# The layer-2 routing of a fused attention and expert kernel: VectorE steps with one operand in PSUM

## The chip, the cores and the metric

The kernel runs on one core of a Trainium2 chip. Five engines of that core work side by side, each through its own list of instructions in order: TensorE (PE; its weight loads are listed as PEld), VectorE (DVE), ScalarE (ACT), GpSimd (POOL), and SyncE (SP), which here only starts DMAs. They wait for one another through semaphores. SBUF is the working memory of 128 partitions. PSUM is the smaller memory into which TensorE writes its results: eight banks of 512 fp32 numbers in each partition, which VectorE and ScalarE also read and write, and POOL and the DMAs do not.

The metric is the device time of one execution in microseconds (us). Before the change it is 998.45 us, the median of three runs (997.95, 998.45 and 1000.06).

## The reference, cut to what matters

Three layers follow each other. The first is attention with a memory term (4 batches, 8 heads, 576 positions, head size 64). Its output, 2304 tokens of 512 numbers, goes through an expert layer in which each token has one of eight experts (512 to 1024 to 512 with a relu). The result goes through a second expert layer in which each token has two. The change concerns how the second layer chooses those two experts. Cut to that:

```python
def _moe2_ref(x, w_gate, w_noise, noise, w1, w2):
    logits = x @ w_gate
    noise_scale = np.log1p(np.exp(x @ w_noise))
    noisy_logits = logits + noise_scale * noise
    top2 = np.argpartition(-noisy_logits, 2, axis=1)[:, :2]
    top2_l = np.take_along_axis(noisy_logits, top2, axis=1)
    top2_w = np.exp(top2_l - top2_l.max(-1, keepdims=True))
    top2_w /= top2_w.sum(-1, keepdims=True) + 1e-09
    for e in range(E):
        for k in range(2):
            mask = top2[:, k] == e
            h = np.maximum(x[mask] @ w1[e], 0.0)
            out[mask] += top2_w[mask, k, None] * (h @ w2[e])
```

## The kernel before, in words

The attention runs first (about 0 to 220 us), its order fixed by a planner in `Tasks` that the change leaves alone. Then `layer1` works through the first expert layer in units of 256 token slots, each unit with the weights of one expert. `full` handles one unit, and `pair` handles two half-filled experts. In this data the order is one `full`, one `pair`, and then seven `full` (the number of pairs and of units is read at run time, in `tc.If` branches). Then `layer2` takes the eight experts of the second layer in turn with up to 640 slots each.

**One unit of layer 1.** Weights and tokens are split into a high and a low part of reduced precision, so each product is three matmuls. `mm1` (L706) makes one of eight blocks of the hidden layer, f = 0 to 7: twelve matmuls (L712 to L714) into a PSUM bank of the kind `h`, then ACT writes the high part `hh` (L715), then DVE writes the low part `hl` from the bank and `hh` (L717). There are two `h` banks, so block f can begin only when `hl` of block f-2 has read its bank. Between the blocks `split_w` (L685) splits the second weight matrix: ACT writes `w2h` (L687), and DVE or POOL writes `w2l` (L688), for f = 3, 5, 7 on DVE and otherwise on POOL. Then `mm2` (L718) makes the output in eight pieces (L722 to L724), between which `split_w1` (L689) splits the next unit's first matrix (L691 on ACT, L692 on DVE and POOL alternately) and `rows` turns the next unit's tokens (L702 to L704).

**The routing of layer 2 rides along.** As soon as a unit's output is known, its tokens' experts of layer 2 are chosen during the next unit. `logits` (L743) computes the two products of the reference (L748, L753, L758) and puts them into the table `L` (L759). `route2` (L869) is a generator of some forty very small DVE steps (16 to 32 numbers in a partition, later 192 to 768) with a few steps of ACT, POOL and PE. `pump` (L760) issues a few of them at a time after each block: five per place in layer 1 (`PUMP`), eight in layer 2 (`PUMP2`). The steps are:

- L878 to L892: softplus of the noise logits by a series, times the noise, plus the logits
- L894 to L899: the two largest, their experts, and the sum `A` of the two one-hot rows
- L901 to L905: PE counts ranks from `A` into a bank of the kind `sm`; this part is held until a given place of the unit
- L906 to L923: the weights of the two experts, each token's slot and column
- L925 to L928: one-hot tables `ol` and `rr` (named `rrm` in the rows) in which slot number and weight are spread out
- L931 and L934: PE multiplies the two, and DVE adds the result to the table `M2`. This last part of a unit is issued after block 1 of the unit behind (`behind`, or at the end of `layer2`'s own chain)

All of these tables stand in SBUF. The order of instructions on each engine is the order in which the code issues them (`manual_schedule`). `Banks` gives each kind of PSUM tile two of the eight banks in turn: `h` 0 and 1, `y` 2 and 3, `tp` (transposes) 4 and 5, `sm` 6 and 7. The attention uses banks 6 and 7 for its own purposes first.

In `layer2` the last unit's routing stands on the way: its `rr` has to be added to `M2` before the list of each expert's tokens is known, so its steps are pumped eight at a time into the first blocks of the first expert.

At L780 (behind the pair) and L785 (behind the last unit) the branches end. There an engine may go on only when the engines it depends on have come to the same place.

Of the kernel before, what the change touches and what calls it, by code (L numbers as in the profile page):

```python
# [9 lines left out]
FT=mybir.dt.float32; FR=mybir.dt.float32r; I32=mybir.dt.int32  # L10
# [275 lines left out]
col=lambda u: 2*u if u<2 else FC+2*(u-2)  # L286
# [12 lines left out]
class Banks:  # L299

    def __init__(s, pool):
        s.all=[pool.tile([128,512],FT,name='b%d'%i) for i in range(8)]
        s.of=dict(h=[0,1],y=[2,3],tp=[4,5],sm=[6,7]); s.n=dict.fromkeys(s.of,0)
    def tile(s, shape, dt, name):
        b=s.all[s.of[name][s.n[name]%2]]; s.n[name]+=1
        return b.rearrange('p (a c) -> p a c',a=shape[1]) if len(shape)==3 else b

class Moe:
    def __init__(s, ctx, tc, ident, consts, areas):
# [40 lines left out]
    def blocks(s, nc, c, areas):  # L350

        def T(j, o, w, name, dt=FT):
            assert o+w<=AREAS[j]
            return nc.alloc_sbuf_tensor_at(name,[128,w],dt,offset=nc.lookup_mloc(areas[j]).addr+4*o).ap()
        cut=lambda j,o,w,name,n,dt=FT:[T(j,o+i*w,w,name+str(i),dt) for i in range(n)]
        V=lambda a,k: a.rearrange('p (k w) -> p k w',k=k)
        K0,K1,X,HL,W2,G,X1,OL=range(8)
        s.w1r=V(T(K0,0,4096,'w1r'),KD); s.w2r=V(T(K0,4096,4096,'w2r'),KF); s.os=cut(K0,8192,512,'os',2)
        s.w1h=V(T(K1,0,4096,'w1h',FR),KD); s.w1l=V(T(K1,4096,4096,'w1l',FR),KD); s.yt=V(T(K1,8192,1024,'yt'),KD); s.rr=c.tile([128,4,256],FR,name='rrm')
        s.xh=V(T(X,0,2560,'xh',FR),KD); s.xl=V(T(X,2560,2560,'xl',FR),KD)  # L360
        s.w2h=cut(W2,0,512,'w2h',KF,FR); s.w2l=cut(W2,4096,512,'w2l',KF,FR)
        H=lambda n: [T(HL,o,KF*n,x+str(n),FR).rearrange('p (f c) -> p f c',f=KF) for o,x in ((0,'hh'),(5120,'hl'))]
        s.hidden=dict(l1=H(UT),l2=H(C2)); s.hh,s.hl=s.hidden['l1']
# [15 lines left out]
        for r in (0,64):  # L379
            nc.gpsimd.affine_select(m4[r:r+64,half-64:],m4[r:r+64,half-64:],pattern=[[-1,64]],compare_op=OP.is_ge,fill=-8e9,base=0,channel_multiplier=1)  # L380
    def banks(s):
        b=s.ps.all; s.bufs.update(s=b[:4],pt=b[4:6],m=b[6:7],ot=b[7:])

    def bias(s, Q, A, ids, mbias):

# [7 lines left out]
        for m in range(nm):  # L393
# [335 lines left out]
    def state(s):  # L729
        nc=s.nc; c=s.c  # L730
        s.run=c.tile([128,E],FT,name='run'); nc.gpsimd.memset(s.run,float(DEAD))
        s.M2=c.tile([128,4,NC2],FT,name='M2'); nc.gpsimd.memset(s.M2,0.0)

        s.NV=NF+NP2+1
        s.sv=c.tile([128,s.NV,2,4],FT,name='sv'); nc.gpsimd.memset(s.sv,8000.0)
        s.val=c.tile([128,s.NV,4,4],FT,name='val'); nc.gpsimd.memset(s.val,0.0)
        s.nz=c.tile([128,3,2,E],FT,name='nz')
        s.L=c.tile([128,2,2*E],FT,name='L'); s.nx=c.tile([128,2,2],FT,name='nx'); s.nxi=c.tile([128,2],I32,name='nxi'); s.lp=c.tile([128,UT],FT,name='lp')
        s.uxi=c.tile([128,2,NF],I32,name='uxi'); s.cnt=c.tile([128,2],I32,name='cnt')
        s.last=c.tile([128,NF],FT,name='last')  # L740
        s.gn=c.tile([128,NF,2],FT,name='gn'); s.gh=c.tile([128,NP2+1,2],FT,name='gh'); s.gni=c.tile([128,NF,2],I32,name='gni')
        s.gsi=c.tile([128,NP2+1,2],I32,name='gsi')
# [126 lines left out]
    def route2(s, wk, ps, u, nt):  # L869

        nc=s.nc; V=nc.vector; G_=nc.gpsimd
        T=lambda name,sh,dt=FT: wk.tile(sh,dt,name=name+('' if nt==2 else '_'))
        cur=s.tabs[:,COLS:COLS+nt]; nz=s.nz[:,2,:nt]; J=2*nt
        G=s.L[:,:nt,:E]; Z=s.L[:,:nt,E:]
        SH=[128,nt,E]
        vals=s.val[:,u,:J]; sv=s.sv[:,u,:,:J]

        e_=T('e_',SH); V.scalar_tensor_tensor(e_,Z,-1.0,Z,op0=OP.mult,op1=OP.min)  # L878
        nc.scalar.activation(e_,e_,AF.Exp); yield
        for k in range(2): G_.tensor_copy(vals[:,nt*k:nt*k+nt,0:2],cur[:,:,0:2])  # L880
# [12 lines left out]
        mx=T('mx2',SH); ix=T('ix2',SH,U32); OH=T('OH',[128,2,nt,E]); id_=T('id_',[128,2,nt])
        for t in range(nt): V.max(mx[:,t],n[:,t]); yield  # L894
        for t in range(nt): V.max_index(ix[:,t],mx[:,t],n[:,t]); yield
        kt=lambda x:x[:,:,0:2].rearrange('p t k -> p k t')
        V.tensor_add(id_,kt(ix),cur[:,None,:,2].to_broadcast([128,2,nt])); yield
        V.tensor_tensor(OH,s.io[:,None,None,:E].to_broadcast([128,2,nt,E]),id_[:,:,:,None].to_broadcast([128,2,nt,E]),op=OP.is_equal); yield
        A=T('A2',SH,BF); V.tensor_add(A,OH[:,0],OH[:,1]); yield 1  # L899
        rp=ps.tile([128,512],FT,name='sm')  # L900
        nc.tensor.matmul(rp[:,0:E],s.trib,A[:,0],start=True,stop=True)  # L901
        if nt==2:
            nc.tensor.matmul(rp[:,E:2*E],s.trib,A[:,1],start=True,stop=False)
            nc.tensor.matmul(rp[:,E:2*E],s.onesb,A[:,0],start=False,stop=True)
        for t in range(nt): nc.tensor.matmul(rp[:,nt*E:(nt+1)*E],s.onesb,A[:,t],start=t==0,stop=t==nt-1)  # L905
        V.tensor_scalar(sv[:,1],id_.rearrange('p k t -> p (k t)'),float(TS),None,op0=OP.mult); yield  # L906
        d=T('d2',[128,nt]); V.tensor_sub(d,mx[:,:,1],mx[:,:,0])
        nc.scalar.activation(d,d,AF.Exp); yield
        rk=T('rk',SH)
        V.tensor_add(rk,rp[:,:nt*E].rearrange('p (t e) -> p t e',t=nt),s.run[:,None,:].to_broadcast(SH)); yield  # L910
        V.tensor_add(s.run,s.run,rp[:,nt*E:(nt+1)*E]); yield
        W=T('w_',[128,J]); V.tensor_scalar(W[:,:nt],d,1.0,1e-9,op0=OP.add,op1=OP.add); yield
        tmp=T('tmp',[128,2,nt,E]); V.tensor_mul(tmp,OH,rk[:,None].to_broadcast([128,2,nt,E])); yield
        V.reciprocal(W[:,:nt],W[:,:nt]); yield
        r=T('r4',[128,J],I32)
        with nc.allow_low_precision(reason='a sum of one whole number and zeros'):
            V.tensor_reduce(r,tmp.rearrange('p k t e -> p (k t) e'),axis=AX.X,op=OP.add)
        yield
        V.tensor_mul(W[:,nt:],W[:,:nt],d); yield
        wh=T('wh',[128,J],FR); G_.tensor_copy(wh,W); G_.tensor_copy(vals[:,:,2],wh.bitcast(FT)); G_.tensor_sub(wh,W,wh.bitcast(FT)); G_.tensor_copy(vals[:,:,3],wh.bitcast(FT))  # L920
        ri=T('ri',[128,2,J],I32); s.lohi(ri,r); yield
        G_.tensor_copy(sv[:,0],r)
        col=T('col',[128,J]); V.scalar_tensor_tensor(col,ri[:,1],float(T2),sv[:,1],op0=OP.min,op1=OP.add); yield  # L923
        ol=s.ol2[:,:J]
        V.tensor_tensor(ol,s.io[:,None,:].to_broadcast([128,J,128]),ri[:,0,:,None].to_broadcast([128,J,128]),op=OP.is_equal); yield  # L925
        oc=wk.tile([128,4,NC2],FT,name='oc')[:,:J]; rr=s.rr[:,:J,:4*NC2].rearrange('p j (a c) -> p j a c',a=4); B=[128,J,4,NC2]
        V.tensor_tensor(oc,s.io[:,None,:NC2].to_broadcast([128,J,NC2]),col[:,:,None].to_broadcast([128,J,NC2]),op=OP.is_equal); yield
        V.tensor_mul(rr,oc[:,:,None].to_broadcast(B),vals[:,:,:,None].to_broadcast(B)); yield 2  # L928
# [218 lines left out]
```

## Time and profile before

| | |
|---|---|
| median of three runs | 998.45 us |
| the profiled execution | 994.96 us, of which 993.2 us are the span from the first to the last instruction |
| PE busy | 949.5 us, 96% of the span |
| PEld busy | 835.0 us, 84% |
| DVE busy | 568.4 us, 57% |
| ACT busy | 487.7 us, 49% |
| POOL busy | 352.8 us, 36% |
| mean granted clock of TensorE | 0.983 of full speed |

An engine's busy time is the sum of its instructions' spans, so a VectorE instruction that has started and stands still counts as busy. "Idle before" in a row is the time in which the engine did nothing ahead of that instruction, and the arrow names what released it. [...] The end of a matmul is modelled: consecutive matmuls of 256 columns start every 0.12 us while each shows 0.28 us, so an idle time that the rows give ahead of such a matmul is 0.16 us shorter than what PE lost.

### The profile page before, as it was taken

The numbers are of one execution on the slowest core, as the hardware profiler recorded it, in microseconds if no ns is written. First come the engines' busy times: TensorE is split into PE (matmuls) and PEld (weight loads), VectorE is DVE, ScalarE is ACT, GpSimd is POOL, SyncE is SP. The second block draws the span as 40 slices with busy tenths as digits, with TensorE's granted clock in tenths as the row PEclk, the third lists the DMA queues.
The fourth block names the chain that finished last, engine by engine and source line by source line (L and its number), as shares of the span: only waits on it lengthen the run. The fifth ranks groups of instructions, "written<-read, shape, count | busy, mean of one in ns | idle before, by whom it ended". The sixth has DMA issues, their size and how long they took to land. (4 is left out here: it accounts for less than half of the span.)

```text
span 993.2 us, 18544 instructions
## 1 busy us (share of the span) xinstructions
PE 949.5 (96%) x6849; PEld 835.0 (84%) x6849; DVE 568.4 (57%) x1675; ACT 487.7 (49%) x1141; POOL 352.8 (36%) x411
## 2 busy tenths in 40 slices
PE   7999999999998999999988999999999999999994
PEld 5888888888876888888867889898989989898983
DVE  8777776899853888888865344253342424244310
ACT  6887878784433555555532243343343434344320
POOL 4222232245634567666644311221313012131111
PEclk9999999999998999999989999999999999999998
DMA  7345856363585455556653334535546353534212
GB/s 208 97 113 186 264 190 194 113 228 101 158 310 186 154 207 195 177 192 210 213 174 128 87 106 135 131 76 135 142 105 153 111 121 106 160 77 110 29 23 35
DMA packets 83842, 144.99 MB, mean 146 GB/s; under 512 B 14480, under 2 KB 32912, under 8 KB 83728
## 3 DMA queue, kind: packets, MB, share of 16 engines
q1 hardware_dynamic: 73168, 117.10, 35.8%
q0 software_dynamic: 10560, 26.47, 13.5%
q8 instruction: 60, 0.98, 0.4%
q14 instruction: 54, 0.44, 0.1%
HBM read 111.65 MB, written 31.97 MB: 145 GB/s over the span
## 5 line engine op out<-in xcount | busy, mean ns | idle before, releaser
L712 PE MATMUL b<-xh,w1h 128*128 128x304 f32 (+3 forms) x800 | 242.1, 303 | 10.4 <-DVEq L785 4.7
L713 PE MATMUL b<-xl,w1h 128*128 128x304 f32 (+3 forms) x800 | 239.5, 299 | 2.8 <-DVEq L780 2.6
L714 PE MATMUL b<-xh,w1l 128*128 128x304 f32 (+3 forms) x800 | 238.6, 298 | 0.8 <-POOLq L780 0.8
L717 DVE SCALAR_TENSOR_TENSOR hl<-b,hh 128x304 fp32r<-128x304 f32 (+3 forms) x200 | 90.3, 452 | 215.2 <-ACT hh L715 215.2
L722 PE MATMUL b<-w2h,hh 128*128 128x512 f32 x464 | 189.1, 407 | 0.0
L724 PE MATMUL b<-w2h,hl 128*128 128x512 f32 x464 | 182.4, 393 | 0.0
L723 PE MATMUL b<-w2l,hh 128*128 128x512 f32 x464 | 181.9, 392 | 0.0
L955 POOL DMA_INDIRECT out_dram<-os,l2s x40 | 63.7, 1593 | 327.6 <-ACT os L954 248.9
L715 ACT ACTIVATE hh<-b 128x304 fp32r<-128x304 f32 (+3 forms) x200 | 81.8, 409 | 187.6 <-PE b L714 187.4
L712 PEld LDWEIGHTS b<-xh,w1h 128*128 128x128 f32 x800 | 153.8, 192 | 18.0 <-DVE hl L717 9.2
L713 PEld LDWEIGHTS b<-xl,w1h 128*128 128x128 f32 x800 | 154.1, 193 | 3.8 <-DVEq L780 2.8
L714 PEld LDWEIGHTS b<-xh,w1l 128*128 128x128 f32 x800 | 154.1, 193 | 1.1 <-POOLq L780 1.1
L724 PEld LDWEIGHTS b<-w2h,hl 128*128 128x128 f32 x464 | 87.6, 189 | 19.7
L723 PEld LDWEIGHTS b<-w2l,hh 128*128 128x128 f32 x464 | 88.2, 190 | 15.7
L722 PEld LDWEIGHTS b<-w2h,hh 128*128 128x128 f32 x464 | 88.0, 190 | 15.6
L151 ACT ACTIVATE p<-sm,l 128x128 f32<-128x128 f32 (+4 forms) x144 | 84.1, 592 | 17.2 <-DVE l L147 17.2
L687 ACT CAST w2h<-w2r 128x512 fp32r<-128x512 f32 x128 | 78.5, 613 | 0.0
L704 DVE TENSOR_TENSOR xl<-b,xh 128x512 fp32r<-128x512 f32 x56 | 38.4, 688 | 69.9 <-ACT xh L703 69.9
L703 ACT CAST xh<-b 128x512 fp32r<-128x512 f32 x56 | 32.8, 587 | 90.1 <-PE b L702 90.1
L954 ACT ACTIVATE os<-b,l2w 128x512 f32<-128x512 f32 x40 | 27.6, 691 | 99.3 <-PE b L724 46.6
L691 ACT CAST w1h<-w1r 128x512 fp32r<-128x512 f32 x128 | 74.7, 619 | 0.0
L692 POOL TENSOR_TENSOR w1l<-w1r,w1h 128x512 fp32r<-128x512 f32 x44 | 59.1, 1352 | 42.3 <-ACT w1h L691 41.2
(500 smaller groups left out, 1536.2 us busy)
## 6 DMA issues: line engine op xcount, KB each, us to landing
w1r<-in_w_dram SPq DMA_DIRECT2D x18, 2048.0 KB, 9.7
w2r<-in_w_dram SPq DMA_DIRECT2D x18, 2048.0 KB, 9.1
xd<-gs SPq DMA_DIRECT2D x24, 260.0 KB, 3.7
xd<-x SPq DMA_DIRECT2D x10, 520.0 KB, 10.1
out_dram<-gs SPq DMA_DIRECT2D x19, 256.0 KB, 3.8
k<-in_k_dram SPq DMA_DIRECT2D x16, 256.0 KB, 4.4
q<-in_q_dram SPq DMA_DIRECT2D x16, 256.0 KB, 3.7
v<-in_v_dram SPq DMA_DIRECT2D x16, 256.0 KB, 4.3
```

The lines of the kernel that those rows point to most:

```text
L151: s.nc.scalar.activation(s.P[b,i,u][:,lh*n:lh*n+n],s.SM[b,i,u][:,lh*n:lh*n+n],AF.Exp,scale=-1.0,bias=L[:,0,c:c+1],accum_out=L[:,1,c:c+1])
L687: nc.scalar.copy(hi[c],raw[:,c])
L691: nc.scalar.copy(s.w1h[:,:,fs],s.w1r[:,:,fs])
L712: nc.tensor.matmul(h[:,:n],s.w1h[:,k,fs],s.xh[:,k,cs],start=k==0,stop=False)
L713: nc.tensor.matmul(h[:,:n],s.w1h[:,k,fs],s.xl[:,k,cs],start=False,stop=False)
L714: nc.tensor.matmul(h[:,:n],s.w1l[:,k,fs],s.xh[:,k,cs],start=False,stop=k==KD-1)
L715: def mm1_a(s, h, f, c0, n): s.nc.scalar.activation(s.hh[:,f,c0:c0+n],h[:,:n],AF.Relu)
L717: cs=slice(c0,c0+n); s.nc.vector.scalar_tensor_tensor(s.hl[:,f,cs],h[:,:n],0.0,s.hh[:,f,cs].bitcast(FT),op0=OP.max,op1=OP.subtract)
L722: nc.tensor.matmul(y,s.hh[:,f,cs],s.w2h[f],start=f==0,stop=False)
L723: nc.tensor.matmul(y,s.hh[:,f,cs],s.w2l[f],start=False,stop=False)
L724: nc.tensor.matmul(y,s.hl[:,f,cs],s.w2h[f],start=False,stop=f==KF-1)
L955: nc.gpsimd.indirect_dma_start(out=out,out_offset=bass.IndirectOffsetOnAxis(ap=si[:,c:c+1],axis=0),in_=o,in_offset=None,compute_op=OP.add)
```

## The change

`s.of['sm']` shrinks to bank 6 alone, and bank 7 becomes a work area for the routing. In it stand `L` (the logits) and the tables `q_`, `acc`, `rk`, `id_`, `col` and `oc` of `route2`. `e_`, `rg`, `q2`, `qn`, `n_`, `OH`, `tmp` and the rest stay in SBUF. Two instructions are new: a copy `zs` of the noise logits in SBUF, so that L878 has one operand in each memory, and a second product `qs`, which puts q times e into SBUF beside the one in PSUM, for the square that follows. The sum `A` of the two one-hot rows becomes a reduction with a single input. The bank that takes the product of L931 is now one of the kind `tp`, because `sm` has only one left.

```diff
-        s.of=dict(h=[0,1],y=[2,3],tp=[4,5],sm=[6,7]); s.n=dict.fromkeys(s.of,0)
+        s.of=dict(h=[0,1],y=[2,3],tp=[4,5],sm=[6]); s.n=dict.fromkeys(s.of,0)
     def tile(s, shape, dt, name):
-        b=s.all[s.of[name][s.n[name]%2]]; s.n[name]+=1
+        b=s.all[s.of[name][s.n[name]%len(s.of[name])]]; s.n[name]+=1
...
-        b=s.ps.all; s.bufs.update(s=b[:4],pt=b[4:6],m=b[6:7],ot=b[7:])
+        b=s.ps.all
+
+        def V(o,*sh):
+            a=b[7][:,o:o+math.prod(sh)]
+            return a if len(sh)==1 else a.rearrange('p (a b) -> p a b',a=sh[0])
+        s.L=V(0,2,2*E); s.pv=dict(q_=V(32,2,E),acc=V(48,2,E),rk=V(64,2,E),id_=V(80,2,2),col=V(84,4),oc=V(128,4,NC2))
+        s.bufs.update(s=b[:4],pt=b[4:6],m=b[6:7],ot=b[7:])
...
-        T=lambda name,sh,dt=FT: wk.tile(sh,dt,name=name+('' if nt==2 else '_'))
+        assert nt==2
+        T=lambda name,sh,dt=FT: s.pv[name] if name in s.pv else wk.tile(sh,dt,name=name)
...
-        e_=T('e_',SH); V.scalar_tensor_tensor(e_,Z,-1.0,Z,op0=OP.mult,op1=OP.min)
+        e_=T('e_',SH); zs=T('zs',SH); V.tensor_copy(zs,Z); V.scalar_tensor_tensor(e_,Z,-1.0,zs,op0=OP.mult,op1=OP.min)
...
-        V.tensor_mul(q,q,e_); yield
-        q2=T('q2',SH); V.tensor_mul(q2,q,q); yield
+        qs=T('qs',SH); V.tensor_mul(qs,q,e_); V.tensor_mul(q,q,e_); yield
+        q2=T('q2',SH); V.tensor_mul(q2,q,qs); yield
...
-        A=T('A2',SH,BF); V.tensor_add(A,OH[:,0],OH[:,1]); yield 1
+        A=T('A2',SH,BF)
+        with nc.allow_low_precision(reason='a sum of zeros and ones'): V.tensor_reduce(A,OH.rearrange('p k t e -> p t e k'),axis=AX.X,op=OP.add)
+        yield 1
...
-        oc=wk.tile([128,4,NC2],FT,name='oc')[:,:J]; rr=s.rr[:,:J,:4*NC2].rearrange('p j (a c) -> p j a c',a=4); B=[128,J,4,NC2]
+        oc=T('oc',[128,4,NC2]); rr=s.rr[:,:J,:4*NC2].rearrange('p j (a c) -> p j a c',a=4); B=[128,J,4,NC2]
...
-        mp=ps.tile([128,512],FT,name='sm')
+        mp=ps.tile([128,512],FT,name='tp')
```

On VectorE nothing else moves past these steps. Between blocks 4 and 5 of the first expert of layer 2, VectorE had this order before the change (`hl640` is the low part of the hidden block, `b0` and `b1` are the `h` banks, `L` the logits):

```order
L717 SCALAR_TENSOR_TENSOR hl640_88<-b0_155,hh640_87 128x224
L878 SCALAR_TENSOR_TENSOR e__8192<-L_231 128x16
L881 SCALAR_TENSOR_TENSOR rg_8197<-L_231,nz_230 128x16
L882 TENSOR_TENSOR rg_8197<-rg_8197,L_231 128x16
L883 TENSOR_SCALAR q__8200<-e__8192 128x16
L884 RECIPROCAL q__8200<-q__8200 128x16
L885 TENSOR_TENSOR q__8200<-q__8200,e__8192 128x16
L886 TENSOR_TENSOR q2_8204<-q__8200 128x16
L887 TENSOR_TENSOR qn_8206<-q__8200,nz_230 128x16
L717 SCALAR_TENSOR_TENSOR hl640_88<-b1_156,hh640_87 128x224
L688 TENSOR_TENSOR w2l5_82<-w2r_60,w2h5_74 128x512
L888 TENSOR_SCALAR acc_8224<-q2_8204 128x16
```

The same place after the change, where `b7` is the work area in PSUM and the line numbers are those of the changed kernel:

```order
L723 SCALAR_TENSOR_TENSOR hl640_88<-b0_155,hh640_87 128x224
L885 COPY zs_8160<-b7_162 128x16
L885 SCALAR_TENSOR_TENSOR e__8159<-b7_162,zs_8160 128x16
L888 SCALAR_TENSOR_TENSOR rg_8166<-b7_162,nz_230 128x16
L889 TENSOR_TENSOR rg_8166<-rg_8166,b7_162 128x16
L890 TENSOR_SCALAR b7_162<-e__8159 128x16
L891 RECIPROCAL b7_162<-b7_162 128x16
L892 TENSOR_TENSOR qs_8171<-b7_162,e__8159 128x16
L892 TENSOR_TENSOR b7_162<-b7_162,e__8159 128x16
L893 TENSOR_TENSOR q2_8174<-b7_162,qs_8171 128x16
L894 TENSOR_TENSOR qn_8176<-b7_162,nz_230 128x16
L723 SCALAR_TENSOR_TENSOR hl640_88<-b1_156,hh640_87 128x224
```

Two instructions are added between the two `hl`; the eight others keep their places, and each has `b7` on one side.

On TensorE the order is the same, instruction for instruction, and only banks change. Around block 1 of the first expert of layer 2 stood (`b6` and `b7` are the two `sm` banks):

```order
L714 MATMUL b1_156<-xh_67,w1l_64 128x224
L712 MATMUL b1_156<-xh_67,w1h_63 128x224
L713 MATMUL b1_156<-xl_68,w1h_63 128x224
L714 MATMUL b1_156<-xh_67,w1l_64 128x224
L931 MATMUL b6_161<-rrm_66,ol2_95 128x256 x4
L753 MATMUL b7_162<-yt_65,wct_247 32x256 x4
L712 MATMUL b0_155<-xh_67,w1h_63 128x224
```

Now stand there, with `b4` one of the two transpose banks:

```order
L720 MATMUL b1_156<-xh_67,w1l_64 128x224
L718 MATMUL b1_156<-xh_67,w1h_63 128x224
L719 MATMUL b1_156<-xl_68,w1h_63 128x224
L720 MATMUL b1_156<-xh_67,w1l_64 128x224
L940 MATMUL b4_159<-rrm_66,ol2_95 128x256 x4
L759 MATMUL b6_161<-yt_65,wct_246 32x256 x4
L718 MATMUL b0_155<-xh_67,w1h_63 128x224
```

The routing's product went from bank 6 to bank 4, and the logits from bank 7 to bank 6.

## Rows read from the trace of the kernel before

**Rows 1.** Waits of PE: line, releaser; us in total, times, longest us

```profile
PE b L712 <- DVE hl L717: 4.1, 9, 0.9
```

**Rows 2.** Windows: busy us of each engine, then clock, DMA share, GB/s

```profile
395.18:422.26 27.08, 26.56 (x182) 23.40 (x182) 22.71 (x62) 15.12 (x34) 18.18 (x24) 1.00 0.57 194
650.00:700.00 50.00, 50.00 (x289) 44.82 (x288) 19.34 (x33) 18.14 (x36) 12.12 (x10) 1.00 0.50 132
```

**Rows 3.** Timeline of PE: start, us, line, operation [idle before, releaser]

```profile
356.84 0.38 PE L712 MATMUL b<-xh,w1h 128*128 128x256 f32 x1 [0.36 <-DVE hl L717]
...
412.15 0.28 PE L714 MATMUL b<-xh,w1l 128*128 128x256 f32 x1
412.95 0.39 PE L712 MATMUL b<-xh,w1h 128*128 128x256 f32 x1 [0.52 <-DVE hl L717]
...
528.78 0.37 PE L712 MATMUL b<-xh,w1h 128*128 128x224 f32 x1 [0.90 <-DVE hl L717]
```

**Rows 4.** Timeline of DVE and ACT ahead of the wait at 412.95

```profile
410.68 1.32 DVE L881 SCALAR_TENSOR_TENSOR rg<-L,nz 128x16 f32<-128x16 f32 x1
412.54 0.36 DVE L717 SCALAR_TENSOR_TENSOR hl<-b,hh 128x256 fp32r<-128x256 f32 x1
...
411.10 0.38 ACT L715 ACTIVATE hh<-b 128x256 fp32r<-128x256 f32 x1
```

**Rows 5.** Timeline of POOL in the same tile

```profile
403.78 1.28 POOL L688 TENSOR_TENSOR w2l<-w2r,w2h 128x512 fp32r<-128x512 f32 x1
409.41 2.55 POOL L688 TENSOR_TENSOR w2l<-w2r,w2h 128x512 fp32r<-128x512 f32 x2
```

**Rows 6.** Timeline of DVE while POOL is in the operation at 403.78

```profile
404.28 0.34 DVE L934 TENSOR_TENSOR M<-M,b 128x192 f32<-128x192 f32 x1
404.66 0.43 DVE L808 TENSOR_SCALAR nx<-M 128x2 f32<-128x2 f32 x1
```

**Rows 7.** Timeline of DVE, POOL and PE at the last branch of layer 1

```profile
504.23 1.22 DVE L906 TENSOR_SCALAR sv<-id__6639 128x4 f32<-128x4 f32 x1
509.58 1.99 DVE L928 TENSOR_TENSOR rrm<-oc,val 128x768 fp32r<-128x768 f32 x1 [0.35 <-POOL val L920]
...
510.71 0.92 POOL L922 CAST sv<-r 128x4 f32<-128x4 int32 x1
511.69 0.19 POOL L775 COPY nz<-nz 128x16 f32<-128x16 f32 x1
...
513.19 0.53 PE L712 MATMUL b<-xh,w1h 128*128 128x224 f32 x1 [4.71 <-DVEq L785]
```

**Rows 8.** Timeline of DVE and PE at the last routing, in layer 2

```profile
526.22 1.28 DVE L882 TENSOR_TENSOR rg<-rg,L 128x16 f32<-128x16 f32 x1
529.24 1.27 DVE L888 TENSOR_SCALAR acc<-q 128x16 f32<-128x16 f32 x1
530.54 0.59 DVE L890 SCALAR_TENSOR_TENSOR acc<-acc,q 128x16 f32<-128x16 f32 x3
536.78 0.96 DVE L928 TENSOR_TENSOR rrm<-oc,val 128x768 fp32r<-128x768 f32 x1 [0.35 <-POOL val L920]
...
533.08 0.17 PE L901 MATMUL b<-A,trib 128*128 128x8 bf16 x1 [2.70 <-DVE A L899]
```

**Rows 9.** Windows behind two waits, columns as in rows 2

```profile
513.20:520.40 7.20, 7.20 (x40) 6.73 (x40) 0.92 (x3) 1.82 (x4) 1.84 (x3) 0.57 0.75 233
533.20:536.20 3.00, 3.00 (x12) 2.42 (x11) 2.64 (x16) 0.20 (x1) 0.83 (x2) 0.50 0.32 61
```

**Rows 10.** Timeline of DVE and PE at the first branch, behind the pair

```profile
313.18 1.97 DVE L928 TENSOR_TENSOR rrm<-oc,val 128x768 fp32r<-128x768 f32 x1
...
317.24 0.58 PE L714 MATMUL b<-xh,w1l 128*128 128x256 f32 x1 [0.80 <-POOLq L780]
```

**Rows 11.** Groups by line: shapes, count, busy us, mean ns, idle before

```profile
L890 DVE SCALAR_TENSOR_TENSOR acc<-acc,q 128x16 f32<-128x16 f32 x30 | 5.2, 172 | 0.7
L910 DVE TENSOR_TENSOR rk<-b,run 128x16 f32<-128x16 f32 x10 | 1.6, 161 | 0.0
```

More of the change, by code (lines that the diff above doesn't have):

```diff
@@ L737, in state @@
         s.nz=c.tile([128,3,2,E],FT,name='nz')
-        s.L=c.tile([128,2,2*E],FT,name='L'); s.nx=c.tile([128,2,2],FT,name='nx'); s.nxi=c.tile([128,2],I32,name='nxi'); s.lp=c.tile([128,UT],FT,name='lp')
+        s.nx=c.tile([128,2,2],FT,name='nx'); s.nxi=c.tile([128,2],I32,name='nxi'); s.lp=c.tile([128,UT],FT,name='lp')
         s.uxi=c.tile([128,2,NF],I32,name='uxi'); s.cnt=c.tile([128,2],I32,name='cnt')
```

## The prediction

> **What bounds the kernel now.** I read the busy times per stretch first, then what PE waits for, then the timelines of DVE and POOL ahead of each of those waits. TensorE is the bound nearly everywhere. In the second expert layer it has no idle time at all, 50.00 us of 50.00; in a steady unit of the first expert layer it is busy 26.56 of 27.08 us [rows 2]. So a faster VectorE is worth only what PE waits for it, and the question is where that is.
>
> One kind of wait comes back in every unit: L712, the first matmul of a block, waits for `hl` (L717), nine times, 4.1 us in all [rows 1]. It is block 7 waiting for the `h` bank of block 5. In the unit that I follow, the last matmul ahead starts at 412.15 and the next at 412.95, with an idle time of 0.52 [rows 3]. Since these matmuls otherwise follow each other every 0.12 us, PE loses 0.68, which is 0.16 more than the idle time. The reason stands on DVE. `hh` of that block is ready at 411.48, but `hl` starts at 412.54, because the routing stands ahead of it in DVE's list and L881 there takes 1.32 us for 16 numbers [rows 4], while such a step takes 0.172 elsewhere [rows 11]. L881 ends at 412.00, and POOL's two splits of `w2l` end at 411.96 [rows 5]. DVE stood still until POOL was through.
>
> Which steps stand still? During POOL's operation from 403.78 to 405.06 [rows 5], L934, which adds a PSUM bank to an SBUF table, ran in 0.34, while L808, a step on two numbers with everything in SBUF, took 0.43 and ended at 405.09, right behind POOL [rows 6]. So a step of one SBUF and one PSUM operand goes through beside POOL, and one with all of it in SBUF may not. The change gives one PSUM operand to most routing steps.
>
> The other waits are at three places. At the last branch of layer 1 PE stands for 4.71 us [rows 7]. At the last routing, in layer 2, it waits 2.70 us for `A` [rows 8]. At the first branch the last wait ahead of it is 0.80 us, for POOL [rows 10].
>
> **The change part by part.** All of it against the profiled execution of 994.96 us (span 993.2, the rest outside it); the median shown is 998.45, so I take the gain from either alike.
>
> *Steady units.* Of the nine waits, the one at 528.78 (0.90) belongs to the last routing, below. The one at 356.84 (0.36) stays, because the step that holds `hl` back there is a split `w2l` on DVE, whose operands remain in SBUF [rows 3]. Seven are left: 4.1 - 0.90 - 0.36 = 2.84, and 0.16 more for each, 4.0 us. They go entirely if `hl` finishes before PE could begin anyway, at 412.15 + 0.12 = 412.27. From L881's start at 410.68 there are four steps to `hl`, and dependent steps come 0.2 us apart (three of L890 in 0.59 [rows 8]); the new copy `zs` adds a fifth. So `hl` may start at 411.7, when `hh` is long ready, and ends 0.36 later at 412.06: 0.2 us to spare. The other stalls of a unit cost PE nothing now, since DVE has caught up before PE asks, and they gain nothing.
>
> *The last routing.* Here the DVE chain itself is what PE waits for. L882 and L888 take 1.28 and 1.27 for 0.17 each [rows 8], 2.2 together, and both lose their stall: L882 reads the logits in PSUM and L888 writes PSUM. The copy `zs` adds 0.2 and the second product 0.1. Gain 1.9 us, which takes up the wait of 0.90 at 528.78 too.
>
> *The last branch.* PE goes on at 513.19, some 1.3 us behind POOL's last step there, at 511.69 to 511.88 [rows 7]. That step is late by two stalls in a row. L906 takes 1.22 for 0.17, which is 1.05 on the way to the weights that POOL works on. L928 takes 1.99 for the 0.96 of an undisturbed one [rows 7, 8], and POOL's cast L922, which should cost what the small copy L775 does (0.19), takes 0.92 and ends when L928 does. That is 1.05 + 0.73 = 1.8 us. Both L906 and L928 read PSUM after the change.
>
> *The first branch.* L928 again takes 1.97 [rows 10] for 0.96, but the splits `w1l` of DVE and POOL that follow still meet each other. I count half of the 1.0, 0.5 us.
>
> *The clock.* [...] If the first wait shrinks to 2.9 and then costs what the wait of 2.70 costs now, 1.6 come back; if the second is cut far enough, 1.5. I take half of each, 1.55 us.
>
> *What it may cost.* Two instructions per routing, ten routings: 0.3 us each, counted above where they lie on the path and hidden by PE's matmuls elsewhere. The bank changes cost nothing: `sm` is refilled only when its reader's result is needed for the refill itself (the second logits product needs the copy of the first), and the `tp` bank that L931 takes was last read a good part of a unit earlier. What no row shows is a DVE step that writes PSUM. From below: steps that read it are no dearer, 161 ns for L910 against 172 for L890 of the same size [rows 11]. From above: a dependent step doubled, 0.2 more. Then the last routing with nine such writes loses 1.8 and what the clock would give it back, the last branch with two 0.4, and the steady units with two 0.4 - 0.2 = 0.2 each, 1.4: 1.8 + 0.75 + 0.4 + 1.4 = 4.4 us less gain. I take nothing, the nearest row's value.
>
> [...]
>
> Sum: 4.0 + 1.9 + 1.8 + 0.5 + 1.55 = 9.8 us. The profiled execution would take 985.2, the median **988.7 us**.
>
> **The rivals.**
>
> *The stall moves on.* What no longer stands still arrives earlier at the next step that has all in SBUF, a split `w2l` or `w1l`, and stands still there, with `hl` behind it. For it: the wait at 356.84, and POOL's two splits in a row [rows 3, 5]. Against it: in the steady unit `hl` comes ahead of the next split. If the seven waits stay and half of the last routing's gain goes, 1.8 + 0.5 + 0.9 = 3.2 are left: 995.2 us.
>
> *Every step that touches PSUM is a little dearer*, by a third of a dependent step, 0.07: some sixteen steps of the last routing lose 1.1, four of the last branch 0.3, and five of each steady unit 0.35 - 0.2 = 0.15, together 1.0. 9.8 - 2.4 = 7.4, 991.1 us. Against it the rows of reading steps. [...]
>
> *Slower: DVE's writes into PSUM are slow to be seen by the next step.* At x us per written step the gain without the clock is 4.0 - 7(2x - 0.2) + 1.9 - 9x + 1.8 - 2x + 0.5 = 9.6 - 25x, so it decides from x = 0.38. At 0.6 the kernel is 5.4 slower: 1003.9 us. Nothing shows such a write; a result that takes three times a whole dependent step would be far from any row.
>
> *The change does not do what it says*: a written or one-sided PSUM operand does not spare the wait. Then the two instructions are hidden or cost a few tenths: 998.5 us. L934 speaks against it.
>
> **How the numbers follow.** Forecast 0.66; stall moves on 0.14; a little dearer 0.08; no effect 0.07; slow writes 0.05. A measurement of this kernel can tell about 0.2% (2 us) from no change. Faster by more than that are the first three, 0.88; within it 0.07; slower 0.05. The range starts at 985, where the clock is regained in full (8.2 + 4.6 = 12.8 us), and goes to 996, behind the case in which the stall moves on; outside lie 0.12 and a little. The forecast alone would lie between 985.6 and 993.1, with its two unknowns at their ends.
>
> **What would show it.** Right: L881, L886 and L906 (by their new numbers) at 0.2 in all units, L928 near 1.0, no wait of L712 for `hl` in the steady units, a period near 26.4 us for 27.08, `A` some two us earlier behind the start of the last routing, PE's stand at the last branch near 3 us. Still long would be the steps that keep two inputs in SBUF, L897 above all. Wrong: written steps more than 0.4 apart, splits of DVE that grew by what the routing lost, or a wait of L931 for the transpose bank.

## The result and the profile after

| | before | after |
|---|---|---|
| median | 999.25 us (997.95 to 1001.98) | 987.65 us (985.52 to 989.80) |
| the profiled execution, its span | 994.96, 993.2 us | 987.47, 985.8 us |
| DVE busy | 568.4 us | 541.9 us, with 20 instructions more |

The ratio is 0.9875, with a 95% interval of 0.9853 to 0.9898. The forecast was 988.7 us. Below, lines of the kernel after have its own numbers: L688 is now L694, L692 is L698, L712 is L718, L714 is L720, L717 is L723, L878 is L885, L881 is L888, L882 is L889, L888 is L895, L897 is L904, L906 is L915, L912 is L921, L922 is L931, L928 is L937.

The waits of PE over the whole span come first (line, releaser, us in total, times, longest).

```profile
PE b L718 <- ACTq L791: 3.7, 1, 3.7
PE b L719 <- DVEq L786: 3.1, 1, 3.1
PE b L189 <- ACT oc L186: 2.2, 1, 2.2
...
PE b L718 <- DVE hl L723: 0.8, 3, 0.4
```

The wait for `hl` fell from 4.1 us in nine to 0.8 in three [rows 1], and from 340 to 500 us PE waits for nothing at all. The unit that answers to the one followed before shows why. This is the timeline of DVE there.

```profile
410.23 0.17 DVE L888 SCALAR_TENSOR_TENSOR rg<-b,nz 128x16 f32<-128x16 f32 x1
...
410.71 0.18 DVE L890 TENSOR_SCALAR b<-e__5588 128x16 f32<-128x16 f32 x1
...
411.10 0.41 DVE L723 SCALAR_TENSOR_TENSOR hl<-b,hh 128x256 fp32r<-128x256 f32 x1
411.55 0.70 DVE L694 TENSOR_TENSOR w2l<-w2r,w2h 128x512 fp32r<-128x512 f32 x1
```

And this is POOL's timeline beside it.

```profile
408.93 2.57 POOL L694 TENSOR_TENSOR w2l<-w2r,w2h 128x512 fp32r<-128x512 f32 x2
411.43 0.86 POOL L887 COPY val<-tabs 128x4 f32<-128x4 f32 x2
```

POOL's pair of splits still runs, until 411.50, but the routing's steps go through beside it in 0.17 each, and `hl` starts at 411.10, ahead of the pair's end. Before, L881 took 1.32 and `hl` started 0.58 after the pair's end [rows 4, 5]. In the window of one whole unit PE is busy for all of it.

```profile
394.84:421.02 26.18, 26.18 (x183) 23.29 (x182) 19.49 (x64) 14.91 (x34) 18.73 (x24) 1.00 0.62 204
```

The period fell from 27.08 [rows 2] to 26.18 us. Some steps still stall: in the groups by line L904, which adds two SBUF tables, takes 0.944 on average, although it writes PSUM, and DVE's splits of `w1` take 0.816, where they took 0.703 before (the second row). They are busy 9.5 us longer in all, so a part of the stalls has moved to them. On the timeline L921, a `tensor_scalar` from SBUF to SBUF, takes 1.26.

```profile
L698 DVE TENSOR_TENSOR w1l<-w1r,w1h 128x512 fp32r<-128x512 f32 x84 | 67.9, 816 | 23.7 <-ACT w1h L697 23.5
...
L692 DVE TENSOR_TENSOR w1l<-w1r,w1h 128x512 fp32r<-128x512 f32 x84 | 58.4, 703 | 26.2 <-ACT w1h L691 26.0
...
L904 DVE TENSOR_TENSOR b<-ix,tabs 128x4 f32<-128x4 uint32 x10 | 9.4, 944 | 0.3
...
500.24 1.26 DVE L921 TENSOR_SCALAR w__6711<-d 128x2 f32<-128x2 f32 x1
```

At the last branch, on DVE, POOL and PE:

```profile
499.65 0.15 DVE L915 TENSOR_SCALAR sv<-b 128x4 f32<-128x4 f32 x1
504.63 0.96 DVE L937 TENSOR_TENSOR rrm<-b,val 128x768 fp32r<-128x768 f32 x1 [0.34 <-POOL val L929]
...
505.75 0.19 POOL L931 CAST sv<-r 128x4 f32<-128x4 int32 x1
506.01 0.20 POOL L781 COPY nz<-nz 128x16 f32<-128x16 f32 x1
...
508.23 0.53 PE L718 MATMUL b<-xh,w1h 128*128 128x224 f32 x1 [3.69 <-ACTq L791]
```

All three steps that were to be shorter are shorter (0.15, 0.96 and 0.19 for 1.22, 1.99 and 0.92 in [rows 7]), but PE stands for 3.69 us, and not for the 2.9 that I worked out: POOL is through 2.02 us before PE goes on, where it was 1.31 before. At the last routing, on DVE and PE:

```profile
521.36 0.17 DVE L889 TENSOR_TENSOR rg<-rg,b 128x16 f32<-128x16 f32 x1
523.51 0.17 DVE L895 TENSOR_SCALAR b<-q 128x16 f32<-128x16 f32 x1
523.72 0.62 DVE L897 SCALAR_TENSOR_TENSOR b<-b,q 128x16 f32<-128x16 f32 x3
...
526.30 0.17 PE L910 MATMUL b<-A,trib 128*128 128x8 bf16 x1 [1.65 <-DVE A L907]
```

Both stalls of [rows 8] are gone, and three dependent steps that write PSUM take 0.62 us, where three in SBUF took 0.59: 0.01 us for each.

One line of the list of waits has nothing to do with the change. At 223.48, at the end of the attention, PE waited 2.21 us for ScalarE's L186, where both ScalarE and VectorE stood still (L186 came after 2.30 us of idle time, VectorE's next step after 1.68). The second run of the same kernel (below) has 0.15 there.

```profile
223.48 0.66 PE L189 MATMUL b<-ident,oc 128*128 128x128 f32 x4 [2.21 <-ACT oc L186]
```

### The profile page after: what moved, and what is told of

Same layout as the page of the kernel before. It is cut to its first block, busy times and chain, and to the rows that moved or that the text cites. A ratio compares the mean times of both kernels' runs of the same rounds, so it can differ in the third digit from the quotient of the medians.

```text
span 985.8 us, 18580 instructions
## 1 busy us (share of the span) xinstructions
PE 946.3 (96%) x6849; PEld 832.9 (84%) x6849; DVE 541.9 (55%) x1695; ACT 487.4 (49%) x1141; POOL 350.4 (36%) x411
## 5 line engine op out<-in xcount | busy, mean ns | idle before, releaser
L718 PE MATMUL b<-xh,w1h 128*128 128x304 f32 (+3 forms) x800 | 241.8, 302 | 6.2 <-ACTq L791 3.7
L720 PE MATMUL b<-xh,w1l 128*128 128x304 f32 (+3 forms) x800 | 238.5, 298 | 0.0
L723 DVE SCALAR_TENSOR_TENSOR hl<-b,hh 128x304 fp32r<-128x304 f32 (+3 forms) x200 | 90.9, 454 | 232.7 <-ACT hh L721 227.2
L718 PEld LDWEIGHTS b<-xh,w1h 128*128 128x128 f32 x800 | 154.1, 193 | 13.2 <-DVE hl L723 5.5
L720 PEld LDWEIGHTS b<-xh,w1l 128*128 128x128 f32 x800 | 154.3, 193 | 0.0
L698 DVE TENSOR_TENSOR w1l<-w1r,w1h 128x512 fp32r<-128x512 f32 x84 | 67.9, 816 | 23.7 <-ACT w1h L697 23.5
```

What stands on the lines that cost most here:

```text
L698: eng.tensor_sub(s.w1l[:,:,fs],s.w1r[:,:,fs],s.w1h[:,:,fs].bitcast(FT))
L718: nc.tensor.matmul(h[:,:n],s.w1h[:,k,fs],s.xh[:,k,cs],start=k==0,stop=False)
L720: nc.tensor.matmul(h[:,:n],s.w1l[:,k,fs],s.xh[:,k,cs],start=False,stop=k==KD-1)
L723: cs=slice(c0,c0+n); s.nc.vector.scalar_tensor_tensor(s.hl[:,f,cs],h[:,:n],0.0,s.hh[:,f,cs].bitcast(FT),op0=OP.max,op1=OP.subtract)
```

## The experiments

My theory was this: a VectorE step with all its operands in SBUF is held until the GpSimd tensor instruction beside it ends (L881, 1.32 us), one operand in PSUM takes it out of that (the same step after, 0.17), and TensorE feels it through the `hl` that stands behind the step. The rivals were that the other edits bring the gain (the reduction, the banks), and that the stall only moves to the next step. All ratios are to the kernel before on the same chip; the periods are the distances of `A`'s first matmul from unit to unit.

| kernel | ratio, 95% interval | period, us | last branch, us |
|---|---|---|---|
| before | 1 | 27.08 | 4.71 |
| the change | 0.9875 (0.9853 to 0.9898) | 26.19 | 3.69 |
| the change again | 0.9889 (0.9874 to 0.9905) | 26.19 | 3.62 |
| all tables in SBUF | 1.0016 (1.0005 to 1.0027) | 27.3 | 4.13 |
| first half in PSUM | 0.9905 (0.9890 to 0.9921) | 26.15 | 3.62 |
| second half in PSUM | 0.9991 (0.9981 to 1.0001) | 27.15 | 4.00 |
| `L` alone | 0.9982 (0.9970 to 0.9995) | 26.8 | 4.32 |
| `q_` and `acc` alone | 0.9992 (0.9983 to 1.0001) | 27.2 | 3.60 |
| before, GpSimd's splits in halves | 0.9976 (0.9962 to 0.9991) | 27.5 | 3.77 |
| before, without GpSimd's three splits | 0.9942 (0.9928 to 0.9955) | 26.15 | 3.54 |
| the change, more in PSUM | 0.9887 (0.9866 to 0.9907) | 26.18 | 3.64 |
| the change, splits in halves | 0.9871 (0.9851 to 0.9892) | 26.19 | 3.35 |

**The change again.** No edit.

> The changed kernel once more, unaltered. It is here for two things: its time beside the three parts below on one chip (987.5, within 1), and the 2.2 us that TensorE lost at 223.48 in the changed kernel's profile (waiting for `oc` of ScalarE's L186, where ScalarE and VectorE both stood still from about 220.8). If that loss is chance, it is absent here (under 0.4 us) and the profiled span is about 983; if it comes with the change, it is here again.

984.33 us against 995.77. The loss at 223 us is absent, and the profiled span is 983.0:

```profile
220.65 0.66 PE L189 MATMUL b<-ident,oc 128*128 128x128 f32 x4 [0.15 <-ACT oc L186]
```

So it does not come with the change, and the first profile understates the gain: 993.2 - 985.8 = 7.4 us there, 993.2 - 983.0 = 10.2 here. It was no single event, though: the profile of the kernel before with GpSimd's splits in halves, below, has the same wait at 2.2 us. Why some executions have it stays open.

**All tables back in SBUF.** The edit, shortened:

```diff
-        s.L=V(0,2,2*E); s.pv=dict(q_=...,acc=...,rk=...,id_=...,col=...,oc=...)
+        s.pv={}
...
+        s.L=c.tile([128,2,2*E],FT,name='L')
```

> All tables of the routing are put back into SBUF; the other edits stay (one bank for `sm`, the `M2` product in `tp`, the copies `zs` and `qs`, the reduction for `A`). Theory (a VectorE step with two SBUF inputs is held up by a GpSimd tensor step beside it, one with an operand in PSUM is not): the time goes back to 1000 (998 to 1002), L889 and L893 take 1.2 us or more again in single units, L937 2.0 us, and TensorE waits for `hl` some 4 us in all. Rival (the gain comes from the other edits: the reduction, or the `sm` and `tp` banks freed of other users): 988, as the changed kernel.

The whole gain is gone, and 0.16% more: `zs` is one further step ahead of `hl`, the period is 0.2 us longer than before, and the waits for `hl` are 6.5 us in all, where I had expected some 4. DVE and POOL of a unit, and PE's waits for `hl`:

```profile
441.79 1.21 DVE L885 SCALAR_TENSOR_TENSOR e__5966<-L,zs 128x16 f32<-128x16 f32 x1
445.14 1.15 DVE L893 TENSOR_TENSOR q<-q__5976,qs 128x16 f32<-128x16 f32 x1
...
440.40 2.56 POOL L694 TENSOR_TENSOR w2l<-w2r,w2h 128x512 fp32r<-128x512 f32 x2
...
PE b L718 <- DVE hl L723: 6.5, 9, 1.3
```

L885 ends at 443.00, POOL's pair at 442.96. The reduction for `A`, the single `sm` bank and the product in `tp` bring nothing by themselves; the place of the tables does. Whether the tables in PSUM would gain as much without them was not run.

**One half alone.** The same line, with `L`, `q_` and `acc` only, and with `rk`, `id_`, `col` and `oc` only.

> Only `L`, `q_` and `acc` in PSUM; `rk`, `id_`, `col` and `oc` in SBUF. Theory with the prediction's terms: the steady units (4.0) and the last routing with its clock (1.9 + 1.5) stay gained, the two branches (1.0 to 2.3) are lost: 989.5 (988.5 to 991); L937 takes 2.0 us, L915 1.1 or more beside a GpSimd split, and TensorE resumes at the last branch 4.7 us after its last matmul. Rival (the second half carries the gain): above 994.

> Only `rk`, `id_`, `col` and `oc` in PSUM; `L`, `q_` and `acc` in SBUF. Theory: only the branches gain: 997.5 (996 to 998.5); TensorE waits for `hl` some 4 us again, and 2.7 us for `A` in the last routing; L937 takes 0.96 us. Rival (the second half carries the gain): below 993.

The first half brings 0.95%, as the theory had it in size. The second brings 0.09%, which its interval does not tell from nothing. One thing was not expected: the first half alone has L937 at its old length, and PE still goes on as early at the last branch as in the whole change.

```profile
L937 DVE TENSOR_TENSOR rrm<-oc,val 128x768 fp32r<-128x768 f32 x10 | 19.0, 1904 | 3.3 <-POOL val L929 3.2
...
507.37 0.52 PE L718 MATMUL b<-xh,w1h 128*128 128x224 f32 x1 [3.62 <-DVEq L791]
```

With the second half alone L937 takes 0.957, and the wait is 4.00; with all tables in SBUF it takes 1.99, and the wait is 4.13. So what L937 takes is worth some 0.1 us at this branch. What differs is when it starts. PE's last matmul ahead of the branch ends 0.1 us before L937 starts in the kernels with `q_` and `acc` in PSUM, and 1.0 to 1.1 us before it in the kernel before and in the parts that leave them in SBUF. From L937's start to PE's next matmul it is 3.0 to 3.6 us in all of these, with L937 at 1.99 as with 0.96. This is read from the kernels side by side; no run moved that start alone.

**`L` alone, and `q_` with `acc` alone.** The same line again.

> Only `L` in PSUM; `q_`, `acc`, `rk`, `id_`, `col` and `oc` in SBUF. Theory (in a steady unit TensorE waits for the one `hl` that stands behind the stalled first steps L885 to L889, which read `L`; the later stalls end beside `hl` that nobody is late for): the waits for `hl` go (under 1 us), the period is 26.2 us, L893 still takes 1.15 us where GpSimd splits, and the ratio to before is 0.991 (0.989 to 0.994). Rival (the stall moves to the next step with two SBUF inputs, and the next `hl` is as late): the period stays at 27 us and the ratio above 0.996.

> The counterpart of the kernel with `L` alone: only `q_` and `acc` in PSUM, `L` and the rest in SBUF. Theory as the kernel with `L` alone left it (one step that stalls ahead of the `hl` is enough, it waits for GpSimd's pair of splits to end whichever step it is): L885 stalls 1.2 us, the steps on `q_` and `acc` take 0.2, the period stays at 27.1 (27.0 to 27.3) and the ratio to before is 1.000 (0.998 to 1.002), so that neither part alone gives what both give together. Rival (the parts add: `L` alone gave 0.998, so this one has the rest of the 0.9905 of the first half): 0.993 or lower.

The expectation for `L` fell, and the rival in it was right: 0.9982. The period, 26.8, lies between the two. DVE of a unit, and POOL:

```profile
440.90 0.17 DVE L889 TENSOR_TENSOR rg<-rg,b 128x16 f32<-128x16 f32 x1
441.13 0.87 DVE L890 TENSOR_SCALAR q__5975<-e__5965 128x16 f32<-128x16 f32 x1
...
442.20 0.36 DVE L723 SCALAR_TENSOR_TENSOR hl<-b,hh 128x256 fp32r<-128x256 f32 x1
...
439.40 2.56 POOL L694 TENSOR_TENSOR w2l<-w2r,w2h 128x512 fp32r<-128x512 f32 x2
```

The steps on `L` pass in 0.17. Then L890, which reads and writes SBUF, stands still until 442.00, and POOL's pair ends at 441.96. `hl` is again behind the end of the pair, 0.24 us now where it was 0.58 before. The counterpart, `q_` and `acc` in PSUM, stalls one step earlier, with the same end:

```profile
437.88 1.22 DVE L885 SCALAR_TENSOR_TENSOR e__5948<-L,zs 128x16 f32<-128x16 f32 x1
...
436.50 2.55 POOL L694 TENSOR_TENSOR w2l<-w2r,w2h 128x512 fp32r<-128x512 f32 x2
```

Against the kernel with all tables in SBUF the two parts save 0.34% and 0.24%, and both together 1.11%. Together they save more than the sum, because in a steady unit one step that stalls ahead of `hl` is enough.

**Without GpSimd's splits beside the routing.** The kernel before, with its tables in SBUF.

```diff
-            s.split_w(s.w2r,s.w2h,s.w2l,f,nc.vector if f in (3,5,7) else nc.gpsimd)
+            if u>2 and f in (2,4,6): nc.scalar.copy(s.w2h[f],s.w2r[:,f])
+            else: s.split_w(s.w2r,s.w2h,s.w2l,f,nc.vector if f in (3,5,7) else nc.gpsimd)
```

> The kernel before, all tables in SBUF, with GpSimd's splits of `w2` for f = 2, 4 and 6 left out in the units from u = 3 on (ScalarE's half of the split stays; the low parts of those three rows are those of unit 2, so that much of the product is another). Theory (it is these GpSimd instructions that hold the first steps of the routing, and nothing else does): L878 to L886 take 0.15 to 0.35 us each, TensorE waits for `hl` under 1 us in all, the period falls from 27.08 to the changed kernel's 26.2 (26.1 to 26.4), and the ratio to before is 0.990 (0.988 to 0.993). Rival (the stall moves once more, to GpSimd's small copies or its splits of `w1` behind them, and TensorE is as late): the period is 26.7 to 27.1 and the ratio above 0.995.

DVE of a unit (L879 is the kernel before's L878, L882 its L881), and PE's waits for `hl` in the whole span:

```profile
410.06 0.17 DVE L879 SCALAR_TENSOR_TENSOR e__5597<-L 128x16 f32<-128x16 f32 x1
410.15 0.17 DVE L882 SCALAR_TENSOR_TENSOR rg<-L,nz 128x16 f32<-128x16 f32 x1
411.16 0.42 DVE L717 SCALAR_TENSOR_TENSOR hl<-b,hh 128x256 fp32r<-128x256 f32 x1
...
PE b L712 <- DVE hl L717: 1.1, 2, 0.9
```

The same steps that took up to 1.32 take 0.17 with everything in SBUF, and the period is 26.15, the changed kernel's within 0.04. That is the cause, shown from its other side. At the last branch the routing's last step starts 0.1 us behind PE's last matmul here too, and the wait is 3.54. The ratio was expected at 0.990 and is 0.9942; I had counted the last routing in, but it stands in layer 2, whose splits this edit does not touch, and its waits of 0.90 and 2.69 are those of before.

**Shorter GpSimd instructions.** The kernel before, and the changed one, with each GpSimd split in two (the splits of `w1` likewise; their lines are left out).

```diff
-        (eng or nc.vector).tensor_sub(lo[c],raw[:,c],hi[c].bitcast(FT))
+        if eng is nc.gpsimd:
+            for j in (0,256): eng.tensor_sub(lo[c][:,j:j+256],raw[:,c,j:j+256],hi[c][:,j:j+256].bitcast(FT))
+        else: (eng or nc.vector).tensor_sub(lo[c],raw[:,c],hi[c].bitcast(FT))
```

> The kernel before, with each split that GpSimd does (1.26 to 1.29 us) issued as two of half the columns; nothing else. It asks what holds the VectorE steps. Theory (a step with two SBUF inputs waits for the end of the GpSimd tensor instruction beside it): a GpSimd half takes 0.65 to 0.7 us, L881 and L886 take at most 0.75 us in place of 1.2 to 1.3, TensorE's waits for `hl` fall from 4.1 us or more to under 1.5, the unit's period from 27.08 to between 26.2 and 26.6 us, and the ratio to before is 0.995 (0.992 to 0.998). Rival 1 (the halves stand back to back and the step passes only when both are done): L881 stays at 1.2 us or more, ratio 1.000. Rival 2 (the stall has nothing to do with GpSimd's instruction): the same, wherever GpSimd's instructions end.

> The changed kernel, with GpSimd's splits in halves as in the first of this set. Theory: the stalls that are left are off TensorE's path, so shorter ones gain nothing: ratio 0.989 (0.987 to 0.991), L921 at 0.75 us or less. Rival 1 (GpSimd's additional instructions make its splits late for the weights): ratio above 0.992. Rival 2 (what is left of the stalls still costs): below 0.986.

In the kernel before, the stall ahead of `hl` did not get shorter but longer. On DVE (L881 here is the kernel before's L878), POOL and PE:

```profile
411.61 2.00 DVE L881 SCALAR_TENSOR_TENSOR e__5665<-L 128x16 f32<-128x16 f32 x1
414.34 0.36 DVE L720 SCALAR_TENSOR_TENSOR hl<-b,hh 128x256 fp32r<-128x256 f32 x1
415.64 0.72 DVE L890 TENSOR_TENSOR qn<-q__5673,nz 128x16 f32<-128x16 f32 x1
...
410.76 2.82 POOL L689 TENSOR_TENSOR w2l<-w2r,w2h 128x256 fp32r<-128x256 f32 x4
415.58 1.46 POOL L689 TENSOR_TENSOR w2l<-w2r,w2h 128x256 fp32r<-128x256 f32 x2 [1.70 <-ACT w2h L687]
...
414.75 0.39 PE L715 MATMUL b<-xh,w1h 128*128 128x256 f32 x1 [1.12 <-DVE hl L720]
```

L881 started at 411.61, when the second half of four (0.70 each) had just begun. It passed at neither of the two borders that followed and ended at 413.61, with the last half at 413.58. Five units show the same 2.00. For this step the theory's sentence on one instruction falls, and rival 1 is right: it waits for the end of the row of instructions that stand back to back.

That is no rule for all steps. In the same unit L890 starts beside the first of two halves and ends after 0.72, near their border, with the second half still running until 417.04. The step that took 1.28 at the last routing [rows 8], L885 here, takes 0.335 in the mean of ten where it took 0.408 before. With whole instructions both happen, too. The first two rows are the kernel before at the pair of [rows 5], the last two the changed kernel.

```profile
410.41 0.35 DVE L878 SCALAR_TENSOR_TENSOR e__5605<-L 128x16 f32<-128x16 f32 x1
410.68 1.32 DVE L881 SCALAR_TENSOR_TENSOR rg<-L,nz 128x16 f32<-128x16 f32 x1
...
271.99 3.57 DVE L904 TENSOR_TENSOR b<-ix,tabs 128x4 f32<-128x4 uint32 x1
271.75 3.77 POOL L698 TENSOR_TENSOR w1l<-w1r,w1h 128x512 fp32r<-128x512 f32 x3
```

L878 got in at the border inside the pair, and L881 behind it was held until the pair's end. L904 stood still through a row of three. What decides whether a step gets in at a border, these runs don't show.

PE's wait in such a unit rose from 0.52 to 1.12, and the period to 27.5, in five of the six periods that I compare below. The first of the six fell from 27.34 to 26.18, though, PE's wait at the last branch from 4.71 to 3.77, and the way to `A`'s matmul in the last routing by 0.7. That is 2.8 us gained against 2.3 lost, which leaves the ratio below 1; the rest of the 0.24% stays open. In the changed kernel the halves make no difference to the time that shows, 0.9871 against 0.9889 with overlapping intervals, and L921 fell to 0.71, as expected.

**More in PSUM.** The changed kernel, with the last stalling steps of the routing put through PSUM.

```diff
-        V.tensor_add(id_,kt(ix),cur[:,None,:,2].to_broadcast([128,2,nt])); yield
+        V.tensor_add(id_,kt(ix),s.pv['pc'][:,None,:].to_broadcast([128,2,nt])); yield
...
-        V.tensor_scalar(W[:,:nt],d,1.0,1e-9,op0=OP.add,op1=OP.add); yield
+        pw=s.pv['pw']; V.tensor_scalar(pw,d,1.0,1e-9,op0=OP.add,op1=OP.add); yield
```

> The changed kernel, and the steps that still stall put through PSUM too: the denominator of the weights in a tile `pw` (L921, 1.27 us), and one input of the addition of the indices (L904, 0.79 us) in a tile `pc`, with two more small instructions. Theory (neither is on TensorE's path: it does not wait at all in the steady units, and at the last branch it resumes no sooner than about 3.6 us after its last matmul whatever the routing's last steps take): L921 and L904 fall to 0.2 us, and the time is that of the changed kernel, ratio to before 0.989 (0.987 to 0.991), the last branch's wait 3.5 to 3.7. Rival (the last branch goes with the routing's end): its wait falls to 2.7, and with it the ratio below 0.988.

In the groups by line the two steps lost their stalls (numbers are one higher here), and PE's wait at the branch stayed:

```profile
L922 DVE TENSOR_SCALAR b<-d 128x2 f32<-128x2 f32 x10 | 1.6, 163 | 1.3 <-ACT d L918 1.3
L905 DVE TENSOR_TENSOR b<-ix,b 128x4 f32<-128x4 uint32 x10 | 1.7, 167 | 0.3
...
508.55 0.52 PE L718 MATMUL b<-xh,w1h 128*128 128x224 f32 x1 [3.64 <-DVEq L791]
```

1.1 and 0.8 us less for two steps of each routing, and nothing gained: no one waited for them. They also show which operand counts. With its output in PSUM and both inputs in SBUF, L904 was held (0.944); with one input in PSUM it is not (0.167). L921 has a single input, and for it an output in PSUM is enough (0.163 for 1.26). No version tried beats the change by more than the intervals allow.

## Why the prediction was right, point by point

The time of the three profiles, taken apart at the same six instructions (start times from the timelines of PE; the first point is L714's matmul of [rows 10], now L720, the last two are those of [rows 7] and [rows 8]):

| stretch, us | before | after | after again | gained |
|---|---|---|---|---|
| to the last of the three matmuls at the first branch | 317.24 | 319.86 | 317.04 | -2.6, 0.2 |
| to `A`'s matmul in the first unit | 23.51 | 22.59 | 23.17 | 0.9, 0.3 |
| six periods | 162.77 | 157.11 | 157.11 | 5.7 |
| to the matmul behind the last branch | 9.66 | 8.67 | 8.61 | 1.0 |
| to `A`'s matmul in the last routing | 19.89 | 18.07 | 16.83 | 1.8, 3.1 |
| to the end | 460.1 | 459.5 | 460.2 | 0.6, -0.1 |

The mechanism was right, and so is the sum: 9.8 us forecast, 10.2 between the profiles of before and after again, 11.6 and 11.4 between the medians of the two comparisons (the profile of before lies 4.3 us under the first one's median). The terms were not all right, and that the sum fits is in part luck: the steady units gave 2.0 us more than I counted, the last branch 0.8 less, and the clock came back whole at one of two places instead of by half at each.

*Steady units, 4.0: too small, 6.0.* The six periods gave 5.7, and the stretch ahead of them, with the seventh wait, 0.3 (the 0.9 of the first run has some clock in it: 0.77 behind the first branch for 0.70, over 7 us). The waits went, all seven, and the one at 356.84 too, which I had kept because a split on DVE stood there. That split had started at 354.19 and stood still until POOL's row was through at 355.89; now it starts at 355.84, just as that row ends, and takes 0.69. And a wait costs more than its idle time plus 0.16. By PE's start times in the unit of [rows 3] the interval at the wait was 0.80 instead of 0.12, the next 0.22 instead of 0.12, which is 0.78 for an idle time of 0.52. Elsewhere in the unit the product L931 kept PE for 0.66 instead of 0.55 until the next matmul: 0.68 + 0.10 + 0.11 = 0.89, the period's 27.08 - 26.19.

*The last routing, 1.9: right.* From the start of the `hl` ahead of the first step to `A`'s matmul it was 533.08 - 525.63 = 7.45 before, and 526.30 - 520.56 = 5.74 after, 1.7 us less.

*The last branch, 1.8: wrong in size, and its step wrong.* I took POOL's last step as what PE waits for, 1.3 us behind it, and counted L906 and L928's cast. Both steps got as short as I said, and the wait fell by 1.0 and not by 1.8. The first half alone, which leaves L937 at 1.9, has the whole of that gain. What the routing's end does behind the start of its last step is hardly on the path; what goes with the gain in all these kernels is that the routing starts this step one microsecond earlier against PE. What PE waits for in the 3.0 to 3.6 us that remain I can't name from the trace: it shows no instruction there.

*The first branch, 0.5: right.* PE's three waits there were 0.88, 2.56 and 0.80 (the last in [rows 10]) and are 0.88 and 3.13, or 0.88 and 3.04 in the second run. The wait for POOL went and most of its idle time came back in the wait ahead of it, 0.2 to 0.3 us less in all. By start times, from the first of the three matmuls to the last, it was 317.24 - 312.92 = 4.32 us before and is 3.82 and 3.81.

*The clock, 1.55: right as a sum, by chance as to the place.* The clock of 0.57 over 7.20 us and of 0.50 over 3.00 us [rows 9] lost 0.43 x 7.2 = 3.1 and 0.50 x 3.0 = 1.5 us. The 1.6 that was to come back at the first place is the difference of the two, and the 1.5 the whole of the second. In windows as in [rows 9], of the kernel after and of its second run:

```profile
508.24:515.44 7.20, 7.20 (x41) 6.66 (x41) 0.98 (x3) 1.82 (x4) 1.85 (x3) 0.58 0.69 221
526.42:529.42 3.00, 3.00 (x18) 2.48 (x16) 2.87 (x16) 0.20 (x1) 1.04 (x3) 1.00 0.38 44
...
505.94:513.14 7.20, 7.20 (x51) 6.66 (x52) 1.04 (x3) 2.71 (x6) 2.01 (x4) 0.76 0.68 225
522.88:525.88 3.00, 3.00 (x12) 2.40 (x10) 2.87 (x16) 0.20 (x1) 1.04 (x3) 0.52 0.31 45
```

In the first run the clock is back at full speed behind the last routing (1.00 for 0.50: 1.5 us) and as low as before behind the last branch (0.58 for 0.57). In the second it is the other way round: 0.76 for 0.57 over 7.2 us gives 1.4 back, and behind the routing it is at the lower level again (0.52). The waits ahead are equal in both, 3.69 and 3.62, 1.65 and 1.65. So the length of the wait alone doesn't set what the clock does after it.

*What writing PSUM costs: nothing, as taken.* 0.01 us a step, above; by the groups by line L897 takes 180 ns for 172, and L919, which was L910, 183 for 161. The rival of the dearer steps, at 0.07 a step, and that of the slow writes fall with it.

*The rival that the stall moves on* was half right. Stalls did move on, to DVE's splits of `w1` (9.5 us) and to L921, but to no place that PE waits for. With `L` alone, and with `q_` and `acc` alone, one stays or moves to where PE does wait for it (L890, 0.87, and L885, 1.22). My reason against it was incomplete. It holds not because `hl` comes ahead of the next split, but because every step between the logits and that `hl` has an operand in PSUM and took 0.17 to 0.27 beside POOL's pair, in the unit followed.

Who stalled beside GpSimd, over all runs: L885 and L893 with two SBUF inputs (1.21 and 1.15 with all tables in SBUF), L904 with two although it writes PSUM (0.944 in the change), L890 and L921 with one input, from SBUF to SBUF (0.87 with `L` alone, 1.26 in the change). Who did not, in the change: L888 with one of its two inputs in PSUM (0.17) and L890 with its output there (0.18). How long it lasts differs: L885 ended 0.04 us behind POOL's pair, but in the run with halves L881 waited 2.00 us, across two borders between instructions of 0.70, and L904 waited 3.57 us through a row of three. What in the chip holds the steps, no run shows.

## What to carry to other kernels

Where a small VectorE step takes a microsecond now and then, look on GpSimd's timeline for the instruction that ends with it. Here one input in PSUM took a step with two inputs out of the way (L888, 0.17 us for 1.32; L904, 0.167 for 0.944), and for a step with a single input an output in PSUM did so too (L890, 0.18 for 0.87; L921, 0.163 for 1.26). That cost 0.01 us a step, in a bank that no other engine used at that time. Do it for every step ahead of the result that TensorE waits for, since one that was left took over most of the stall (L890 with `L` alone, 0.87, period 26.8) or all of it (L885 with `q_` and `acc` alone, 1.22, period 27.2), and for none behind it. Take what a wait of TensorE costs from the start times around it and not from its idle time: here the idle time was 0.52 and the start times gave 0.78.

## What the runs showed that was not expected

POOL's steps stood still beside DVE's as well. Beside DVE's split at 411.55 POOL's two small copies took 0.86 us (the POOL row of the first section); in the run without GpSimd's three splits, where VectorE was idle beside them (L881 there is L887 after the change), they took 0.31:

```profile
409.05 0.31 POOL L881 COPY val<-tabs 128x4 f32<-128x4 f32 x2
```

Splitting a GpSimd instruction made it dearer as well, 2.82 us for the four halves where the pair took 2.55 [rows 5], and the head of the routing stood still for 2.00 us instead of 1.32 in five units, though other steps stood for a shorter time.
